# Rows of o of two tiles in one visit across block borders, with finer positions in a planned order

## The chip, the cores and the metric

The kernel runs on one core of a Trainium2 chip. The metric is the device time of one execution in microseconds (us), the median of several runs. A profiled execution has a time of its own; its span, from the first to the last instruction, is a little shorter than that time.

## The reference

Linear attention with a norm by head, and then an MLP with softplus:

```
kv = einsum('bhsd,bhse->bhde', k, v)          # 8 batches, 8 heads, 576 positions, head size 64
o  = einsum('bhsd,bhde->bhse', q, kv)
rms = sqrt(mean(o * o, axis=-1) + 1e-06)
x  = (o / rms * g_norm) -> (4608 tokens, 512)
h  = x @ w_in                                 # 512 -> 2048
out = softplus(h) @ w_out                     # 2048 -> 512
```

q, k, v and g_norm are float32, w_in and w_out float64. The output is float32.

## The kernel before

**Arithmetic.** A float32 matmul is made of fp32r matmuls on three pieces of each operand (a high part, a rest, and a scaled difference). Weights, x and softplus(h) are split into such pieces by ACT and DVE, and TensorE (PE) adds three products in its accumulators.

**Stages.** Tokens come in 36 tiles of 128. A batch has 576 tokens, four and a half tiles, so that some tiles hold rows of two batches.

- `kv_of(b)` loads k and v of one batch and makes kv on PE (L672, five pieces for each batch: four pairs of loads and a tail); ACT copies the result.
- `rows(t)` makes a tile of o. q is turned (by PE at L752 for batches 0 and 1, by DVE at L727 later), PE makes the rows (`out_rows`, L696, 16 matmuls of 64*64 for each tile; the profile counts each twice), ACT squares them (L769), DVE sums (L700), POOL takes the root (L703, L704), DVE multiplies (L708). x is then turned, for the first 12 tiles on PE (`turn_x`, L714) and later on DVE (L795), and stored to DRAM (L779, L799). For the first six tiles, x is also split at once (L616, L619, L622).
- Phase 0 works on 12 blocks of three tiles (384 tokens) and the first chunks of the hidden layer, four chunks of 128 for the first four blocks and six for the others, 64 steps in all. A step has `mm1` (L839, 12 matmuls of 384 columns), softplus (L861), the split into `gv` (L863, L850, L854) and `mm2` (L846, nine matmuls of 512 columns, three for each tile). The partial output goes to DRAM (L891, L906).
- Phases 1 and 2 work on nine blocks of 512 tokens and pairs of chunks, 48 steps in all. They use a form with seven products in place of eight: `units_of` prepares sums of x, `both` prepares sums of weights, `wide_step` has seven products of six matmuls (L1026, 256 columns), the softplus and split (L1053, L1075, L1083, L1086, L1089) and eight `mm2` of three matmuls (L1096). Phase 2 adds the partial outputs of the phases before (L885) and writes the result.
- Weights arrive as float64 and are converted by ACT and six DVE instructions (L414 to L440, with L410 and L427 on ACT), then split (`split_weight`, L477 to L505). Weights that are needed later are spilled to DRAM (L458) and loaded again.

**What sets the order.** The kernel does not issue instructions as the source stands. Each piece of work is a `Task` with an engine, a cost, the tasks it needs, buffers that it takes and gives, and a position. `Plan.order` builds the whole order before anything is issued: on each engine it takes, of the tasks that can start within a small window, the one with the lowest position. So the position is a rank, and the engine's queue is fixed when the program is built. On PE, `rows` and `kv` tasks are of a kind of their own, and the planner keeps tasks of one kind together when several are ready; a small cost is charged for a change of kind. Where PE would stand idle early on, the planner puts in a filler, `warm` (L1177), a matmul on the identity.

A DMA has a `behind`: it is not issued before the mm1 of a given step is. All data DMAs but two are issued from SP.

The lines that the change and the prediction touch:

```
# which tile joins the rows of the tile before it (12 = BY_PE, TB = 3 tiles in a block)
second = t >= BY_PE and t % TB == 1
if second:
    rows_done[t - 1].after.extend(turned + need)
a = o_task = add("PE", 484, out_rows, turned + need, pos - second, [o], [qT], kind="rows", follows=rows_done.get(t - 1))
```

With `second`, the tile before also waits until this tile's q is turned and its kv is there, so that both can be done in one visit. `x_pos(t)` gives a tile's position, `EARLY`, `CONVERT`, `FETCH`, `LATER`, `SPLIT`, `TAKEN` and `MM2` hold the positions and offsets of loads, conversions, splits and matmuls.

Of the kernel before, what the change touches and what calls it, by code (L numbers as in the profile page):

```python
# [18 lines left out]
P = 128  # L19
# [181 lines left out]
def kernel(  # L201
# [44 lines left out]
    STEPS = [(ph, n, p) for ph in (1, 2) for n in range(n_wide) for p in PAIRS[ph - 1][n]]  # L246
    LAST = 2

    P0 = [-48.16, -11.59, -36.23, -9.34, -21.88, -6.03, 0.48, 3.73, -72.34, -30.1, -41.26, -15.18, -39.67, -26.8, -3.81, 5.27, 8.4, -26.81, 14.38, 10.02, 8.24, 12.88, -11.53, 5.44, 1.19, 33.13, -14.12, 6.15, 11.68, 7.45]
    CONVERT, FETCH, EARLY, LATER = P0[:8], P0[8:16], P0[16:27], P0[27:]  # L250
    P1 = [49.25, 55.64, 61.04, 40.09, 109.45, 133.28, 49.73, 28.85, 72.45, 98.22, 131.85, 140.31]
    P2 = [24.13, 36.89, 36.77, 47.57, 55.58, 67.77, 58.81, 116.43, 78.93, 120.62, 44.24, 19.49, 49.95, 77.41, 122.0, 83.32, 80.75, 86.17, 164.23, 141.39, -6.45]
    P3 = [1.62, 1.24, 5.47, 0.83, 2.68, 2.58, 4.22, 2.0, 2.57, 2.99, 3.06, 1.5, 1.16, 0.45, 2.4, -0.72]
# [330 lines left out]
    def load_q(b):  # L584


        q_slots[b], q_loads[b] = slot("qa"), []
        pos = x_pos(first_tile[b] + 1) - EARLY[7]

        def run(a, p):  # L590
            if not (a or p):
                new(q_slots[b], [P, NP * S])
            e, c = divmod(a, 2)
            nc.sync.dma_start(
                out=q_slots[b].tile[BL * a:BL * (a + 1), p * S:(p + 2) * S].rearrange("j (i d) -> j i d", d=BL),
                in_=q[b, e * NP + p:e * NP + p + 2, :, BL * c:BL * (c + 1)].rearrange("p (i j) d -> j (p i) d", j=BL))

        for a in range(4):
            for p in range(0, NP, 2):
                q_loads[b].append(add("SP", 500, lambda a=a, p=p: run(a, p), (), pos + 0.1 * (2 * a + p // 2),  # L600
                                      [q_slots[b]] if not (a or p) else [], [], 1095, behind=int(pos) - 3,
                                      follows=q_loads[b][-1] if a or p else None))

    def split(t, x, ready, pos):
# [33 lines left out]
    def x_pos(t):  # L638

        n = t // TB  # L640
        return t * EARLY[0] + EARLY[1] if n == 0 else first_step["block", n] - (EARLY[2] if n == 1 else EARLY[3]) + t % TB

    def kv_of(b):

        pos = x_pos(first_tile[b]) - (EARLY[4] if b else EARLY[5])
        bank = slot(f"s{b}" if b < 2 else "tp")
        last = first = None
        MAIN = 4 * P  # L650
        for p in range(NP + 1):
# [11 lines left out]
            lds = [add("SP", 500, lambda src=src, s=s, load=load: load(src, s), (), pos - EARLY[6] + 0.5 * p, [s], [],  # L663
                       650 if tail else 850, behind=int(pos - 2) - 3) for src, s in ((k, ks), (v, vs))]

            def run(ks=ks, vs=vs, p=p, tail=tail):
                kv = new(bank, [P, NP, D]) if p == 0 else bank.tile
                for i in range(4):
                    for e in range(2):
                        l, r = (x.tile[:, i + e * NP] if tail else x.tile[:, e, i] for x in (ks, vs))  # L670

                        nc.tensor.matmul(kv[e * D:(e + 1) * D, i if tail else p], lhsT=l, rhs=r,  # L672
                                         start=(p == 0 and i == 0), stop=tail, skip_group_check=True)
            if b >= 2 and (p % 2 or tail):
                first.after.extend(lds)
            last = add("PE", 470, run, lds + ([last] if b < 2 else []), pos + 0.5 * p, [bank] if p == 0 else [], [ks, vs], kind="kv",
                       follows=last if b >= 2 else None)
            if p % 2 == 0 and not tail:
                first = last
        kv_ready[b] = [add("ACT", 400, lambda: nc.scalar.copy(kvs[b % 2], bank.tile), [last] + o_tasks.get(b - 2, []),  # L680
                           pos + 2.5, [], [bank])]

    def rows(t):
# [38 lines left out]
        for b, r0, n, s0 in parts(t):  # L722
            if b >= 2:
                if b not in q_slots:
                    load_q(b)
                turned.append(add(
                    "DVE", 690 if n == P else 420, lambda b=b, r0=r0, n=n, s0=s0: nc.vector.transpose(  # L727
                        out=part_of_qT(n, r0),
                        in_=q_slots[b].tile.rearrange("k (p s) -> k p s", p=NP)[:, :, s0:s0 + n]),
                    q_loads[b], pos - 1, [qT] if not r0 else [], [q_slots[b]], follows=turned[-1] if turned else None))  # L730
                continue

            if 0 not in q_slots:
                q_slots[0] = slot("qa")
            at_qa = n == P and b == 0
            q_s = q_slots[0] if at_qa else slot("n")

            def load(b=b, n=n, s0=s0, q_s=q_s, at_qa=at_qa):
                if q_s.tile is None:
                    new(q_s, [P, NP * S] if at_qa else [P, H, D])  # L740
                for e in range(2):
                    nc.sync.dma_start(out=natural(q_s, at_qa)[:n, e::2], in_=halves(q[b, :, s0:s0 + n], e))  # L742

            def natural(q_s, at_qa):
                if not at_qa:
# [9 lines left out]
            ld = add("SP", 900, load, (), pos - EARLY[7], [q_s] if not at_qa or t == 0 else [], [], 1220 * n // P,  # L755
                     behind=int(pos) - 3, follows=first_load[0] if t and at_qa else None)
            first_load.append(ld)
            a = add("PE", 440, turn_q, [ld], pos - 1, [tp], [q_s])
            turned.append(add("ACT", 590, lambda n=n, r0=r0, tp=tp: nc.scalar.copy(part_of_qT(n, r0), tp.tile[:, :, :n]),
                              [a], pos - 1, [qT] if not r0 else [], [tp], follows=turned[-1] if turned else None))  # L760
        need = [u for pt in parts(t) for u in kv_ready[pt[0]]]
        second = t >= BY_PE and t % TB == 1
        if second:
            rows_done[t - 1].after.extend(turned + need)
        a = o_task = add("PE", 484, out_rows, turned + need, pos - second, [o], [qT], kind="rows", follows=rows_done.get(t - 1))
        rows_done[t] = a
        for pt in parts(t):
            o_tasks.setdefault(pt[0], []).append(a)
# [149 lines left out]

    def units_of(ph, n):

        at = starts[first_of[ph, n]] - LEAD
        held = {}
        for j, us in enumerate(GROUPS):
            pos = at + APART * j - (EARLIER if ph == 1 else 0)
# [79 lines left out]
    def wide_step(k):  # L1004
# [101 lines left out]
        for c in range(2):  # L1106
            for i in range(TW):
                slot_pos = b + PACE + MM2[TW * c + i]
                a2 = add("PE", 700, lambda c=c, i=i: mm2(c, i),
                         [a] + factors_done[1, 2 * p + c] + ([seeds[i]] if i in seeds and not c else []) +  # L1110
                         ([before[i]] if c else []), slot_pos, [mine[i]] if first and not c and ph < LAST else [], [gv] + ([outs[c]] if final else []))
                before[i] = a2
                if last and c:
                    leave(ph, TW * n + i, mine[i], a2, slot_pos)
# [30 lines left out]
    for c in range(KF):  # L1145
        for j in (2 * c, 2 * c + 1):
            if c < OWN:
                pos = CONVERT[j] if c < 4 else LATER[c - 4] + LATER[2] * (j % 2)
                weight(j, pos, FETCH[j] if c < 4 else pos, int(pos) - 3)
# [63 lines left out]
```

## Time and profile before

| | |
|---|---|
| median of 3 runs | 881.16 us (880.52 to 881.33) |
| profiled execution, its own time | 881.73 us |
| its span | 878.6 us |
| granted TensorE clock | 0.998 |
| PE busy | 858.5 us (98%) |
| DVE busy | 704.3 us (80%) |
| ACT busy | 519.5 us (59%) |
| POOL busy | 80.1 us (9%) |
| DMA, mean over the span | 190 GB/s |

An engine's busy time is the union of its instructions; a share is that time over the span. For PE the ends of matmuls are modelled and neighbours overlap, so the times from one start to the next are used where a duration matters. In the timeline, each line has the start, the length, the engine, the source line, what is written and read, and how many equal instructions were merged; the bracket at the end is the idle time before it and what ended it. "Filler" in this document means the matmuls at L1177.

### The profile page before, as it was taken

The numbers are of one execution on the slowest core, as the hardware profiler recorded it, in microseconds if no ns is written. First come the engines' busy times: TensorE is split into PE (matmuls) and PEld (weight loads), VectorE is DVE, ScalarE is ACT, GpSimd is POOL, SyncE is SP. The second block draws the span as 40 slices with busy tenths as digits, with TensorE's granted clock in tenths as the row PEclk, the third lists the DMA queues.
The fourth block names the chain that finished last, engine by engine and source line by source line (L and its number), as shares of the span: only waits on it lengthen the run. The fifth ranks groups of instructions, "written<-read, shape, count | busy, mean of one in ns | idle before, by whom it ended". The sixth has DMA issues, their size and how long they took to land.

```text
span 878.6 us, 16974 instructions
## 1 busy us (share of the span) xinstructions
PE 858.5 (98%) x6463; PEld 757.6 (86%) x6463; DVE 704.3 (80%) x992; ACT 519.5 (59%) x979; POOL 80.1 (9%) x79
## 2 busy tenths in 40 slices
PE   7799999999999999999999999999999999999998
PEld 4578888888898899888988988898888888888996
DVE  6888888887887988898988877789787867787863
ACT  5675555544444467766667645555767654665554
POOL 0442143023113200000000000000000000000000
PEclk9999999999999999999999999999999999999999
DMA  9998999969683774446654645645463743777764
GB/s 252 240 220 207 304 210 254 224 174 226 185 169 125 193 213 137 157 129 205 223 165 140 197 133 175 214 151 174 144 180 120 252 154 125 237 228 222 227 191 129
DMA packets 239633, 167.06 MB, mean 190 GB/s; under 512 B 106304, under 2 KB 198464, under 8 KB 239552
## 3 DMA queue, kind: packets, MB, share of 16 engines
q1 hardware_dynamic: 239392, 165.99, 67.0%
q8 instruction: 50, 0.82, 0.4%
q14 instruction: 31, 0.25, 0.1%
q10 hardware_dynamic: 160, 0.00, 0.0%
HBM read 112.98 MB, written 52.95 MB: 189 GB/s over the span
## 4 chain that ended last, share of the span: by engine, by line
PE 91%; DMA 2%; DVE 2%; ACT 2%; SPq 1%; issue 1%; POOL 0%; DVEq 0%; ACTq 0%
PE banks L1096 30%; PE banks L1026 26%; PE banks L846 15%; PE banks L839 15%; PE banks L696 2%; PE banks L672 2%; DMA raw<-in_moe_w_in_dram 1%; SPq L742 1%; DMA early<-in_q_dram 1%; PE banks L714 1%; DMA loads<-in_v_dram 1%; DVE half L708 0%; ACT w L778 0%; POOL r L704 0%; SPq L661 0%
## 5 line engine op out<-in xcount | busy, mean ns | idle before, releaser
L1096 PE MATMUL banks<-pieces,gv 128*128 128x512 f32 x552 | 173.0, 394 | 0.0
L1026 PEld LDWEIGHTS banks<-units,pieces 128*128 128x128 f32 x1212 | 159.1, 190 | 11.0 <-ACT banks L1071 2.0
L1026 PE MATMUL banks<-units,pieces 128*128 128x256 f32 x1212 | 166.2, 282 | 0.7 <-ACT banks L1067 0.4
L846 PE MATMUL banks<-pieces,gv 128*128 128x512 f32 x576 | 146.4, 397 | 0.0
L839 PE MATMUL banks<-units,pieces 128*128 128x384 f32 x768 | 145.6, 338 | 0.1
L839 PEld LDWEIGHTS banks<-units,pieces 128*128 128x128 f32 x768 | 135.0, 188 | 5.1 <-ACT pieces L505 0.2
L846 PEld LDWEIGHTS banks<-pieces,gv 128*128 128x128 f32 x576 | 105.8, 188 | 20.9
L1096 PE MATMUL banks<-pieces,g_False 128*128 128x512 f32 x276 | 108.3, 392 | 0.4 <-DVE g_False L1089 0.4
L1096 PEld LDWEIGHTS banks<-pieces,gv 128*128 128x128 f32 x552 | 95.1, 189 | 13.4 <-DVE banks L885 0.4
L1086 DVE TENSOR_TENSOR gv<-g_True,gv 128x1024 fp32r<-128x1024 f32 x48 | 58.7, 1223 | 40.9 <-ACT gv L1083 40.7
L861 ACT ACTIVATE half<-banks 128x384 f32<-128x384 f32 x64 | 31.4, 491 | 88.9 <-PE banks L839 86.6
L1096 PE MATMUL banks<-w,gv 128*128 128x512 f32 x216 | 67.7, 394 | 0.0
L1053 ACT ACTIVATE g_True<-banks 128x256 f32<-128x256 f32 x96 | 36.8, 384 | 49.1 <-PE banks L1026 47.9
L704 POOL TENSOR_TENSOR r<-r,half 128x8 f32<-128x8 f32 x36 | 65.1, 1808 | 3.0
L1096 PEld LDWEIGHTS banks<-pieces,g_False 128*128 128x128 f32 x276 | 51.8, 188 | 12.5 <-ACT banks L1071 0.8
L989 DVE TENSOR_TENSOR units<-loads,units 128x1024 fp32r<-128x1024 f32 x42 | 51.2, 1220 | 11.4 <-ACT units L986 11.2
L1089 DVE SCALAR_TENSOR_TENSOR g_False<-gv 128x1024 fp32r<-128x1024 f32 x48 | 58.7, 1224 | 1.4
L1075 DVE TENSOR_TENSOR g_True<-banks,g_True 128x512 f32<-128x512 f32 x48 | 33.1, 690 | 24.8 <-PE banks L1026 18.9
L992 DVE SCALAR_TENSOR_TENSOR units<-units 128x1024 fp32r<-128x1024 f32 x42 | 51.4, 1223 | 1.6
L1083 ACT ACTIVATE gv<-g_True 128x1024 fp32r<-128x1024 f32 x48 | 51.0, 1062 | 1.5
L850 DVE TENSOR_TENSOR gv<-half,gv 128x384 fp32r<-128x384 f32 x64 | 35.1, 549 | 20.3 <-ACT gv L863 19.4
L891 ACT ACTIVATE m<-banks 128x512 f32<-128x512 f32 x72 | 42.2, 596 | 15.4 <-PE banks L1096 9.5
(116 smaller groups left out, 1347.9 us busy)
## 6 DMA issues: line engine op xcount, KB each, us to landing
loads<-x SPq DMA_DIRECT2D x180, 128.0 KB, 2.8
part<-m SPq DMA_DIRECT2D x72, 256.0 KB, 3.0
m<-part SPq DMA_DIRECT2D x72, 256.0 KB, 3.3
loads<-form SPq DMA_DIRECT2D x45, 256.0 KB, 3.0
form<-loads SPq DMA_DIRECT2D x36, 256.0 KB, 2.8
raw<-in_moe_w_in_dram SPq DMA_DIRECT2D x16, 512.0 KB, 5.2
loads<-in_k_dram SPq DMA_DIRECT2D x32, 256.0 KB, 4.9
loads<-in_v_dram SPq DMA_DIRECT2D x32, 256.0 KB, 5.0
```

Of the source, the lines that this page charges most:

```text
L704: nc.gpsimd.tensor_tensor(out=r.tile, in0=r.tile, in1=half, op=ALU.pow)
L839: nc.tensor.matmul(hp, lhsT=w_in.tile[:, i, kd * P:(kd + 1) * P], rhs=xv.tile[:, i, kd], start=(m == 0), stop=(m == 3 * KD - 1))
L846: nc.tensor.matmul(mine[i].tile, lhsT=gv.tile[:, m, i * P:(i + 1) * P], rhs=w_out.tile[:, m], start=(c == cs[0] and m == 0), stop=(c == cs ...
L891: a = add("ACT", 690 if ph == LAST else 600, lambda: nc.scalar.activation(new(ot, [P, d_model]), bank.tile, func=AF.Copy, scale=scale if p ...
L989: nc.vector.tensor_tensor(out=part_of(1, F32R), in0=xl.tile if m > 1 else xl.tile[:, 0], in1=part_of(0), op=ALU.subtract)
L992: nc.vector.scalar_tensor_tensor(out=part_of(2, F32R), in0=part_of(1), scalar=-RADIX, in1=part_of(0), op0=ALU.mult, op1=ALU.add)
L1026: nc.tensor.matmul(place(q), lhsT=w[:, m, at:at + P], rhs=dst.tile[:, m, v, kd] if u < 6 else dst.tile[:, m, kd], start=(u == 0 and not m ...
L1053: nc.scalar.activation(dst, src, func=AF.Softplus, scale=1.0 + E)
L1083: nc.scalar.activation(gvt(0, F32R), gt(), func=AF.Copy, scale=DOWN)
L1086: nc.vector.tensor_tensor(out=gvt(1, F32R), in0=gt(), in1=gvt(0), op=ALU.subtract)
L1089: nc.vector.scalar_tensor_tensor(out=gt(F32R), in0=gvt(1), scalar=-RADIX, in1=gvt(0), op0=ALU.mult, op1=ALU.add)
L1096: nc.tensor.matmul(mine[i].tile, lhsT=(gvt(m, F32R) if m < 2 else gt(F32R))[:, c, i * P:(i + 1) * P], rhs=outs[c].tile[:, m], start=fresh ...
```

## The change

It does three things. First, the rule for which tile joins the one before it: it was the middle tile of each block of three, from tile 12 on; now it is each odd tile from 13 on, so that pairs (12, 13), (14, 15) and so on run across the borders of blocks, and the pair's position is that of its first tile. Second, a tile's position within its block is spread over the block's steps, and lists of offsets are added (`P4` for each tile, `P5` for each batch's kv and q loads, `P6` for each block's units, `P7` for single loads of the first two batches and tiles). All old constants are replaced. Third, three small rules: `behind` of loads is no longer rounded, and in phases 1 and 2 each first `mm2` of a block's step also names the one before it on the same tile of the block as something to wait for.

```diff
+    P4 = [-30.17, -6.08, 16.93, -33.9, ...
+    P5 = [1.24, -5.69, -2.28, 1.58, ...
+    P6 = [-0.39, 4.6, -0.28, -2.24, ...
+    P7 = [-23.78, -17.98, -11.85, ...
-    P1 = [49.25, 55.64, 61.04, 40.09, 109.45, 133.28, 49.73, 28.85, 72.45, 98.22, 131.85, 140.31]
-    P2 = [24.13, 36.89, 36.77, 47.57, 55.58, 67.77, 58.81, 116.43, 78.93, 120.62, 44.24, 19.49, 49.95, 77.41, 122.0, 83.32, 80.75, 86.17, 164.23, 141.39, -6.45]
+    P1 = [48.8, 48.65, 66.31, 74.64, 125.35, 131.27, -11.31, 54.26, 67.75, 469.13, 282.82, 195.86]
+    P2 = [22.14, 35.93, 25.02, 37.31, 52.38, 81.67, 74.61, 116.65, 106.27, 111.35, 100.82, -152.23, 99.52, 221.41, 428.54, -173.95, 119.58, -155.43, 317.87, 212.07, -7.69]
...
-        pos = x_pos(first_tile[b] + 1) - EARLY[7]
+        pos = x_pos(first_tile[b] + 1) - EARLY[7] + P5[B + b]
...
-                                      [q_slots[b]] if not (a or p) else [], [], 1095, behind=int(pos) - 3,
+                                      [q_slots[b]] if not (a or p) else [], [], 1095, behind=pos - 3.5,
...
-        return t * EARLY[0] + EARLY[1] if n == 0 else first_step["block", n] - (EARLY[2] if n == 1 else EARLY[3]) + t % TB
+        return P4[t] + t * EARLY[0] + EARLY[1] if n == 0 else P4[t] + first_step["block", n] - (EARLY[2] if n == 1 else EARLY[3]) + t % TB * (len(CHUNKS[n]) // TB)
...
-        pos = x_pos(first_tile[b]) - (EARLY[4] if b else EARLY[5])
+        pos = x_pos(first_tile[b]) - (EARLY[4] if b else EARLY[5]) + P5[b]
...
-        second = t >= BY_PE and t % TB == 1
+        second = t > BY_PE and t % 2 == 1
         if second:
             rows_done[t - 1].after.extend(turned + need)
-        a = o_task = add("PE", 484, out_rows, turned + need, pos - second, [o], [qT], kind="rows", follows=rows_done.get(t - 1))
+        a = o_task = add("PE", 484, out_rows, turned + need, x_pos(t - second), [o], [qT], kind="rows", follows=rows_done.get(t - 1))
...
-        at = starts[first_of[ph, n]] - LEAD
+        at = starts[first_of[ph, n]] - LEAD + P6[n_wide * (ph - 1) + n]
...
-                         ([before[i]] if c else []), slot_pos, [mine[i]] if first and not c and ph < LAST else [], [gv] + ([outs[c]] if final else []))
+                         ([before[i]] if c or not first else []), slot_pos, [mine[i]] if first and not c and ph < LAST else [], [gv] + ([outs[c]] if final else []))
```

`P0` and `P3`, the remaining lists of positions, get new values in the same way. After the change all source lines below the lists stand four lines lower.

More of the change, by code (lines that the diff above doesn't have):

```diff
@@ L247 @@
     LAST = 2
-    P0 = [-48.16, -11.59, -36.23, -9.34, -21.88, -6.03, 0.48, 3.73, -72.34, -30.1, -41.26, -15.18, -39.67, -26.8, -3.81, 5.27, 8.4, -26.81, 14.38, 10.02, 8.24, 12.88, -11.53, 5.44, 1.19, 33.13, -14.12, 6.15, 11.68, 7.45]
+    P0 = [-45.94, -26.77, -11.8, 0.28, -29.91, -5.64, -2.86, 3.84, -103.4, -98.98, -69.3, -76.66, -68.5, -24.67, -23.22, -34.97, 8.15, -43.02, 7.47, 9.69, 7.18, 18.16, -12.1, 4.75, 1.0, 95.98, -6.45, 6.38, 7.69, 5.17]
+    P4 = [-30.17, -6.08, 16.93, -33.9, -22.35, -28.91, -17.33, -7.12, -9.75, -2.59, 0.87, 2.93, -12.14, -3.26, 0.98, 3.76, 7.8, -3.0, -2.25, 7.68, 20.89, 50.27, -0.5, -0.13, 26.66, 22.67, -11.61, -5.55, 2.74, 0.64, -0.48, 1.34, 0.64, 1.68, -8.4, -1.37]
+    P5 = [1.24, -5.69, -2.28, 1.58, 5.58, 0.43, 5.83, -7.56, 3.01, -2.95, 3.18, 1.42, -14.52, 0.57, -1.29, -1.34]
+    P6 = [-0.39, 4.6, -0.28, -2.24, -0.01, 1.05, 1.77, -3.9, -2.15, 0.85, 1.85, -1.74, 6.34, -2.44, -0.13, 3.82, 7.89, 0.51]
+    P7 = [-23.78, -17.98, -11.85, -14.93, 0.41, 1.61, 7.35, 2.7, -25.02, -6.6, -15.2, -4.48, -2.14, 0.64, 2.93, 0.97, 4.67, 5.36, 3.33, 6.57, -10.37, 2.36, -14.11, -9.89, -7.11, 12.91, -2.89, 14.55, 12.59, 9.35]
     CONVERT, FETCH, EARLY, LATER = P0[:8], P0[8:16], P0[16:27], P0[27:]
-    P1 = [49.25, 55.64, 61.04, 40.09, 109.45, 133.28, 49.73, 28.85, 72.45, 98.22, 131.85, 140.31]
-    P2 = [24.13, 36.89, 36.77, 47.57, 55.58, 67.77, 58.81, 116.43, 78.93, 120.62, 44.24, 19.49, 49.95, 77.41, 122.0, 83.32, 80.75, 86.17, 164.23, 141.39, -6.45]
-    P3 = [1.62, 1.24, 5.47, 0.83, 2.68, 2.58, 4.22, 2.0, 2.57, 2.99, 3.06, 1.5, 1.16, 0.45, 2.4, -0.72]
+    P1 = [48.8, 48.65, 66.31, 74.64, 125.35, 131.27, -11.31, 54.26, 67.75, 469.13, 282.82, 195.86]
+    P2 = [22.14, 35.93, 25.02, 37.31, 52.38, 81.67, 74.61, 116.65, 106.27, 111.35, 100.82, -152.23, 99.52, 221.41, 428.54, -173.95, 119.58, -155.43, 317.87, 212.07, -7.69]
+    P3 = [3.0, 2.86, 5.84, -16.31, 1.53, 3.03, 3.55, -20.64, 3.15, 2.55, 1.38, 1.52, 1.27, 0.75, 2.42, -1.39]
     SPLIT = {p: (P1[i], P1[6 + i]) for i, p in enumerate((2, 3, 4, 5, 6, 7))}
@@ L661, in load @@
                 nc.sync.dma_start(out=new(s, [P, 2, 4, D]), in_=src[b, p::NP, :MAIN].rearrange("h (s i) d -> s h i d", i=4))
-            lds = [add("SP", 500, lambda src=src, s=s, load=load: load(src, s), (), pos - EARLY[6] + 0.5 * p, [s], [],
-                       650 if tail else 850, behind=int(pos - 2) - 3) for src, s in ((k, ks), (v, vs))]
+            lds = [add("SP", 500, lambda src=src, s=s, load=load: load(src, s), (), pos - EARLY[6] + 0.5 * p + (P7[2 * (5 * b + p) + of_v] if b < 2 else 0), [s], [],
+                       650 if tail else 850, behind=pos - 5.5) for of_v, (src, s) in enumerate(((k, ks), (v, vs)))]
             def run(ks=ks, vs=vs, p=p, tail=tail):
@@ L754, in rows @@
             tp = turn_q.__defaults__[-1]
-            ld = add("SP", 900, load, (), pos - EARLY[7], [q_s] if not at_qa or t == 0 else [], [], 1220 * n // P,
-                     behind=int(pos) - 3, follows=first_load[0] if t and at_qa else None)
+            ld = add("SP", 900, load, (), pos - EARLY[7] + P7[20 + t], [q_s] if not at_qa or t == 0 else [], [], 1220 * n // P,
+                     behind=pos - 3.5, follows=first_load[0] if t and at_qa else None)
             first_load.append(ld)
@@ L1148 @@
                 pos = CONVERT[j] if c < 4 else LATER[c - 4] + LATER[2] * (j % 2)
-                weight(j, pos, FETCH[j] if c < 4 else pos, int(pos) - 3)
+                weight(j, pos, FETCH[j] if c < 4 else pos, pos - 3.5)
             else:
```

## The prediction

> **What bounds the kernel now.** I read the page's busy times first, then busy time by stage, then PE's timeline and its waits.
>
> ```profile
> PE 858.5 (98%) x6463; PEld 757.6 (86%) x6463; DVE 704.3 (80%) x992; ACT 519.5 (59%) x979; POOL 80.1 (9%) x79
> ```
>
> ```profile
> 0.00:48.00 48.00, 34.61 (x429) 24.74 (x430) 35.89 (x64) 29.54 (x58) 10.16 (x15) 0.96 0.96 244
> 48.00:78.00 30.00, 28.69 (x330) 23.92 (x329) 26.17 (x45) 19.52 (x40) 11.22 (x10) 1.00 0.88 228
> 78.00:364.00 286.00, 285.50 (x2536) 253.21 (x2536) 238.15 (x409) 155.19 (x304) 58.67 (x54) 1.00 0.79 195
> 364.00:875.00 511.00, 509.68 (x3171) 455.73 (x3169) 404.07 (x477) 314.81 (x581) 0.00 (x0) 1.00 0.58 180
> ```
>
> The columns are stage, length, busy time of PE, PEld, DVE, ACT, POOL, then clock, DMA share, GB/s. From 78 us to the last matmul PE idles 0.50 + 1.32 = 1.8 us of 797. There the end is the sum of what PE is given, and another engine counts only if it makes PE wait. Before 48 us the DMA share is 0.96 and PE is idle for 13.4 us; also, part of its "busy" time is filler (L1177, 18.2 us in all, a matmul on the identity that the planner puts into gaps).
>
> What PE's small jobs cost shows in start-to-start times (start, length, operation):
>
> ```profile
> 176.62 2.26 PE L846 MATMUL banks<-pieces,gv 128*128 128x512 f32 x9
> 178.82 1.16 PE L696 MATMUL banks<-early,w 64*64 64x64 f32 x64
> 179.91 2.37 PE L839 MATMUL banks<-units,pieces 128*128 128x384 f32 x12
> 182.12 2.24 PE L846 MATMUL banks<-pieces,gv 128*128 128x512 f32 x9
> 184.20 2.27 PE L839 MATMUL banks<-units,pieces 128*128 128x384 f32 x12
> ...
> 271.61 4.35 PE L839 MATMUL banks<-units,pieces 128*128 128x384 f32 x24
> 275.89 0.69 PE L696 MATMUL banks<-early,w 64*64 64x64 f32 x32
> 276.52 2.36 PE L839 MATMUL banks<-units,pieces 128*128 128x384 f32 x12
> 278.72 4.33 PE L846 MATMUL banks<-pieces,gv 128*128 128x512 f32 x18
> ```
>
> L846 x9 lasts 2.08 us when L839 follows (182.12 to 184.20), but 2.20 when rows of o (L696) follow; L839 x12 lasts 2.21 after a visit, 2.10 elsewhere. Two tiles in one visit (x64) take 1.09, one tile (x32) 0.63. So a visit costs 0.10 on entry and 0.11 on exit: one tile 0.84 us, two tiles 1.30, and **two singles made one save 2 x 0.84 - 1.30 = 0.38 us**; with 0.62 for a single, the commoner value, 0.35. I take 0.35.
>
> The waits on PE after 78 us are four short ones:
>
> ```profile
> PE banks L696 <- ACT half L769: 0.4, 1, 0.4
> PE banks L1026 <- ACT banks L1067: 0.4, 1, 0.4
> PE banks L1096 <- DVE g_False L1089: 0.4, 1, 0.4
> PE banks L1026 <- ACT g_True L1050: 0.3, 1, 0.3
> ```
>
> The start-up, PE's timeline:
>
> ```profile
> 44.70 0.69 PE L672 MATMUL banks<-loads 128*64 128x64 f32 x16 [1.17 <-DMA loads<-in_v_dram]
> ...
> 47.12 0.69 PE L696 MATMUL banks<-early,w 64*64 64x64 f32 x32
> 47.74 2.36 PE L839 MATMUL banks<-units,pieces 128*128 128x384 f32 x12
> ...
> 60.88 0.73 PE L1177 MATMUL banks<-ident_r 128*128 128x512 f32 x2
> 62.49 0.66 PE L714 MATMUL banks<-ident_r,half 128*128 128x128 f32 x4 [0.88 <-ACT half L769]
> ```
>
> The first mm1 (L839) stands at 47.74, behind the last kv of batch 1, which waited for DMA until 44.70. After it fillers and waits still take 1.61 us (60.88 to 62.49), 0.92 and 0.33 us (until 77.53) and 0.16: 3.0 in all.
>
> **What the Trainium skill says.** "TensorEngine Tiling (Array Packing)", Key Properties: changing the tiling mode drains TensorE. The trace agrees: rows run as 64*64 between 128*128 work, and the two changes cost the 0.10 and 0.11 us above. "TensorE: Matmul & The Clock Gate", section "Wait — 56ns, not 53.3ns?", gives 215.7 ns between 512-column matmuls; here 2.10 / 9 = 233 ns, and I use that. "DMA: Bandwidth & Descriptors", "Why small descriptors are slow", names a fixed cost per packet. The trace agrees; two short stretches of DMA, q-heavy (12.1 to 14.0 us) and nearly without q (14.8 to 19.0):
>
> ```profile
> DMA packets 1005, 0.40 MB, mean 209 GB/s; under 512 B 811, under 2 KB 1005, under 8 KB 1005
> ...
> DMA packets 1189, 1.48 MB, mean 352 GB/s; under 512 B 121, under 2 KB 1068, under 8 KB 1189
> ```
>
> **The change part by part.**
>
> *Rows of o.* In the built instruction order of both kernels I count runs of L696 on PE. All 36 tiles take 28 visits before, 23 after. The last 27 tiles (from tile 9 on), which lie in the part where PE never idles, take 20 visits before and 16 after: 4 x 0.35 = **-1.4 us**. Tiles 2 and 3 are merged too, but ahead of the first mm1, where PE idles: 0. Tile 5's visit moves ahead of the first mm1; that takes 0.83 from the work after it and adds it to the start-up. What is late next is ACT's Square of both tiles, two of 0.60 us back to back; two o slots hold both.
>
> *Other PE work.* mm1, mm2, products, kv visits (20) and x transposes (12 visits) are equal in number. Runs of product and wide mm2 number 171 and 168 before, 170 and 169 after. I priced all runs from the first mm1 on by the durations above: 821.5 us before, 819.1 after, difference 2.4: 1.4 + 0.83 and 0.2 of small moves. (The measured stretch, 47.74 to 874.74, is 827.0 = 821.5 + 3.0 + 1.8 + 0.7 unassigned.)
>
> *Start-up loads (SP's queue, DMAs included).* Both kernels move the same 10.24 MB up to the last k and v of batch 1. But before, two q tiles (7 and 8, 2 x 256 KB) stand ahead of them, and after, w_in of chunk 3 (512 KB) stands there. At 209 and 352 GB/s: 2.5 against 1.5 us. So that kv is ready near 43.7 instead of 44.7. Behind it after: kv 1.1, q transpose 0.4, rows 0.7, x transpose 0.45, rows 0.65, six fillers of 0.33: first mm1 at about 49.1, **+1.35 us** against 47.74. From there on two fillers (0.66) remain, and I expect about 1.0 of waiting for tile 4's x (6.7 us from its rows to its transpose in the trace of before, 47.12 to 53.78): 1.7 instead of 3.0, **-1.3 us**. The kinds of both terms are sure, their sizes to 1 us each.
>
> *DVE.* The first g-split ends (L854) as the 85th DVE instruction, not the 74th: 11 more, about 7.1 us at 0.45 to 0.73 each. DVE before has done that much at about 62 us. PE after reaches the mm2 that needs it at about 63.5 us. So it is hidden, with 1.5 us to spare; beyond that it costs one for one.
>
> *Loads' gates, weight conversions, units, the added order among mm2 runs in phase 2.* All are positions in queues. The added dependency holds PE against PE, which is in order anyway: 0. Nothing is added to or taken from DVE (992 both) or ACT. The longest DVE work between two g-splits falls from 9.8 to 7.8 us in the 384-token part and from 15.9 to 11.3 in the 512-token part (counts by row durations), which speaks for no new wait. The 1.8 us of waits after 78 us may vanish or double: +-1.8; I take 0.
>
> Sum: -2.4 + 1.35 - 1.3 = **-2.35 us**. The profiled execution took 881.73 us (878.6 of span, 3.1 around it), so 879.4 for it; the median of the runs is 0.57 lower, 881.16, so **878.8**. The tail (last matmul 874.74, ACT 0.69, store, end 878.6) doesn't change.
>
> **The rivals.** (1) *As above*, 877.8 to 879.9, chance 0.46: within it the start-up terms move by 1 us. (2) *The waits after 78 us go too*: -2.35 - 1.8 = 877.0. For it: the one of 0.43 at 188 us lies between single visits, of which there are fewer. Against: three are in the 512-token part or near the end, which is hardly reordered. Chance 0.20. (3) *The start-up gives it back*: the DMA advance isn't there (+1.0) or DVE's 11 instructions come out late (1 us); only the visits are left or less: 880 to 881, no measurable change. For it: DVE is 75% busy before 48 us, 87% until 78. Chance 0.27. (4) *Slower*: the conversions of weight chunks 7, 11 and 13 get positions far below zero, so that each weight's six DVE instructions (0.43 + 3 x 0.69 + 0.43 + 0.69 = 3.6 us) run as soon as it lands, ahead of a waiting g-split. PE's cover is one mm1 and one mm2, 4.2 us, less ACT's and DVE's 2.1 us for the split itself: 2.1 us. Above that PE waits; six such weights at 1.5 us, half of them hit: +4.5 - 2.35, so 883.3. Against it: the shorter stretches above. Chance 0.07. That the change doesn't do what it says is excluded by the count 28 to 23.
>
> **How the numbers follow.** A measurement of this kernel can tell about 0.2% (1.76 us) from no change, so faster means under 879.4. Case 2 is faster whole, of case 1 nearly all (0.43), case 3 is the same with a little of case 1, case 4 slower. Faster 0.64, same 0.29, slower 0.07. The range takes in cases 1 to 3: 876.8 to 881.1.
>
> **What would show it.** Right: L696 in 16 visits from tile 9 on, each double 1.09; first mm1 near 49; last filler before 79 us; PE idle after that under 2 us. Wrong: waits of PE on DVE at L846 (case 3 if at 60 to 65 us, case 4 if between 80 and 360), or a last kv of batch 1 still at 44.7.

## The result and the profile after

The changed kernel takes **874.38 us** (median of four runs, 873.61 to 875.38); the kernel before took 880.84 us on the same chip (four runs, 880.11 to 881.33). The ratio is 0.9928, 95% interval 0.9911 to 0.9945: faster by 6.5 us. I had forecast 878.8 us with a range of 876.8 to 881.1. The sign was right; the size was not, and the range missed.

The profiled execution took 873.68 us, with a span of 871.7 us and a granted clock of 0.994. The time around the span was 2.0 us, and it was 3.1 us in the profiled execution before; therefore I compare spans and positions inside them, not the two profiled times.

The busy times of the page after:

```profile
PE 858.2 (98%) x6464; PEld 761.2 (87%) x6464; DVE 703.9 (81%) x992; ACT 521.4 (60%) x979; POOL 78.3 (9%) x79
```

PE's busy time is that of before to 0.3 us, although the span is 6.9 us shorter. As a total it says nothing about the change: fillers are in it, and the modelled ends of matmuls cover short stalls. The stages say more (stage, length, busy time of PE, PEld, DVE, ACT and POOL, then clock, DMA share, GB/s):

```profile
0.00:48.00 48.00, 39.95 (x471) 29.91 (x472) 38.33 (x69) 31.68 (x61) 11.62 (x18) 0.89 1.04 264
48.00:78.00 30.00, 28.54 (x358) 23.74 (x357) 25.80 (x45) 20.46 (x41) 10.95 (x12) 1.00 0.95 238
78.00:364.00 286.00, 286.00 (x2494) 254.94 (x2493) 243.19 (x417) 156.72 (x309) 55.73 (x51) 1.00 0.81 197
364.00:868.00 504.00, 503.75 (x3147) 452.62 (x3145) 396.55 (x464) 311.91 (x570) 0.00 (x0) 1.00 0.57 179
```

From 78 us on PE idles 0.25 us, where it idled 1.8. The list of waits, which had four entries for PE in that stretch, has none. Before 48 us DVE does 38.33 us of work, 2.4 more than before, and DMA moves 264 GB/s, not 244.

Visits of rows of o are as counted: 16 from tile 9 on. A double one in PE's timeline (start, length):

```profile
72.80 1.16 PE L700 MATMUL banks<-early,w 64*64 64x64 f32 x64
73.89 2.35 PE L843 MATMUL banks<-units,pieces 128*128 128x384 f32 x12
```

From start to start that is 1.09 us, as in the kernel before. The start-up in the same timeline:

```profile
40.85 0.69 PE L676 MATMUL banks<-loads 128*64 128x64 f32 x16
...
45.35 1.66 PE L1181 MATMUL banks<-ident_r 128*128 128x512 f32 x6
46.85 2.27 PE L843 MATMUL banks<-units,pieces 128*128 128x384 f32 x12
```

The last kv pair of batch 1 (L676) no longer waits for a DMA and stands at 40.85, where I expected 43.7. The six fillers are there as predicted, and the first mm1 (L843) stands at 46.85, not at 49.1 as predicted, nor at 47.74 as before.

**Where the time came from.** I take PE's timeline from start to start and price each run of equal matmuls by the durations in the prediction. What is left over in a stretch is waits and fillers. This account of one profiled execution is called its ledger below.

| | before | after | difference | predicted |
|---|---|---|---|---|
| first mm1 starts at | 47.74 | 46.85 | -0.89 | +1.35 |
| PE work from there on, priced | 821.53 | 819.08 | -2.45 | -2.4 |
| fillers and waits until 78 us | 3.34 | 3.02 | -0.32 | -1.3 |
| left over, 78 to 364 us | 0.46 | -0.22 | -0.68 | 0 |
| left over, from 364 us | 1.67 | -0.84 | -2.51 | 0 |
| last matmul ends at | 874.74 | 867.88 | -6.86 | -2.35 |

The negative values are the error of the prices, about 1 us in 790. With prices taken anew, as medians over several of the traces, the two left-over terms come out as -0.3 and -2.8: their sum, 3.1 to 3.2 us, is firm, and how it divides between the two stretches is known to about 0.4. The work term is the count of the built order at the same prices as in the prediction, so its agreement shows no more than that the order was counted rightly; the price of a visit is tested in e12 below. The term that I had set to zero holds 3.2 us, and the start-up 1.2 us (first mm1 and fillers together) where I had a sum of zero.

The 2.5 us from 364 us on lie in the runs of product and of wide mm2 (L1030, L1100). By the ledger five stalls of the kernel before, at 84, 187, 368, 675 and 684 us, hold 2.6 of the 3.2 us; the changed kernel has none over 0.2 us there. Two of the five, each in its run (in the bracket the idle time and its releaser):

```profile
373.79 0.98 PE L1026 MATMUL banks<-units,pieces 128*128 128x256 f32 x6 [0.41 <-ACT banks L1067]
...
676.29 2.41 PE L1026 MATMUL banks<-units,pieces 128*128 128x256 f32 x18 [0.26 <-ACT g_True L1050]
```

Around the first, 60 matmuls of product took 7.82 us from start to start, 0.67 more than their price; the bracket shows 0.41. The second names 0.26, and its run of 72 lost 0.56. After the change, products stand back to back from the first one on:

```profile
362.49 3.02 PE L1030 MATMUL banks<-units,pieces 128*128 128x256 f32 x24
365.35 1.58 PE L1030 MATMUL banks<-early,w 128*128 128x256 f32 x12
```

### The profile page after: what moved, and what is told of

The parts are those of the page before. It is cut to its first block, busy times and chain, and to the rows that moved or that the text cites. A ratio compares the mean times of both kernels' runs of the same rounds, so it can differ in the third digit from the quotient of the medians.

```text
span 871.7 us, 17016 instructions
## 1 busy us (share of the span) xinstructions
PE 858.2 (98%) x6464; PEld 761.2 (87%) x6464; DVE 703.9 (81%) x992; ACT 521.4 (60%) x979; POOL 78.3 (9%) x79
## 4 chain that ended last, share of the span: by engine, by line
PE 94%; DMA 2%; DVE 2%; ACT 1%; POOL 1%; issue 0%; SPq 0%; POOLq 0%; DVEq 0%; ACTq 0%
PE banks L1100 30%; PE banks L1030 28%; PE banks L850 16%; PE banks L843 15%; PE banks L700 2%; PE banks L676 2%; DMA loads<-in_k_dram 1%; DMA loads<-in_v_dram 1%; PE banks L1181 1%; PE banks L718 0%; POOL r L708 0%; DVE half L712 0%; PE banks L756 0%; SPq L403 0%; DVE units L623 0%
## 5 line engine op out<-in xcount | busy, mean ns | idle before, releaser
L1100 PE MATMUL banks<-pieces,gv 128*128 128x512 f32 x696 | 217.9, 394 | 0.0
L843 PE MATMUL banks<-units,pieces 128*128 128x384 f32 x768 | 145.8, 338 | 0.0
L850 PE MATMUL banks<-pieces,gv 128*128 128x512 f32 x576 | 145.5, 396 | 0.0
L843 PEld LDWEIGHTS banks<-units,pieces 128*128 128x128 f32 x768 | 135.1, 188 | 5.1
L1100 PEld LDWEIGHTS banks<-pieces,gv 128*128 128x128 f32 x696 | 121.2, 189 | 18.1
L1100 PE MATMUL banks<-pieces,g_False 128*128 128x512 f32 x348 | 136.4, 392 | 0.1
L1030 PEld LDWEIGHTS banks<-units,pieces 128*128 128x128 f32 x948 | 126.9, 190 | 8.3 <-ACT banks L1075 1.3
L1030 PE MATMUL banks<-units,pieces 128*128 128x256 f32 x948 | 132.5, 282 | 0.0
L850 PEld LDWEIGHTS banks<-pieces,gv 128*128 128x128 f32 x576 | 106.3, 187 | 21.0
L1100 PEld LDWEIGHTS banks<-pieces,g_False 128*128 128x128 f32 x348 | 65.4, 188 | 15.3 <-DVE g_False L1093 0.6
L1030 PEld LDWEIGHTS banks<-units,w 128*128 128x128 f32 x396 | 52.5, 189 | 2.8
L1030 PE MATMUL banks<-units,w 128*128 128x256 f32 x396 | 54.8, 281 | 0.0
L990 ACT ACTIVATE units<-loads 128x1024 fp32r<-128x1024 f32 x42 | 44.4, 1058 | 17.0 <-PE banks L1030 11.0
```

The source lines that it names most:

```text
L843: nc.tensor.matmul(hp, lhsT=w_in.tile[:, i, kd * P:(kd + 1) * P], rhs=xv.tile[:, i, kd], start=(m == 0), stop=(m == 3 * KD - 1))
L850: nc.tensor.matmul(mine[i].tile, lhsT=gv.tile[:, m, i * P:(i + 1) * P], rhs=w_out.tile[:, m], start=(c == cs[0] and m == 0), stop=(c == cs ...
L990: nc.scalar.activation(part_of(0, F32R), xl.tile if m > 1 else xl.tile[:, 0], func=AF.Copy, scale=DOWN)
L1030: nc.tensor.matmul(place(q), lhsT=w[:, m, at:at + P], rhs=dst.tile[:, m, v, kd] if u < 6 else dst.tile[:, m, kd], start=(u == 0 and not m ...
L1100: nc.tensor.matmul(mine[i].tile, lhsT=(gvt(m, F32R) if m < 2 else gt(F32R))[:, c, i * P:(i + 1) * P], rhs=outs[c].tile[:, m], start=fresh ...
```

## The experiments

All were timed in five rounds beside the kernel before. Two kinds were made. In the first the planned order is kept and single tasks are moved in it. In the second one part of the positions is set back, or put alone into the kernel before, and the whole is planned again. Below, "start-up" is the start of the first mm1 plus fillers and waits until 78 us: 51.08 before, 49.87 after. Ledgers are of the profiled executions. In the cuts of code, "..." marks what is left out, and the comments are added.

### What a visit costs

**e12_visits_split.** The changed kernel in its own order; wherever a main PE task follows a double visit from tile 12 on, the second tile's rows go behind that task.

```diff
-    for t in plan.order():
+    planned = plan.order()
+    tasks = list(planned)
...
+    for one, two, then in zip(on_pe, on_pe[1:], on_pe[2:]):
+        if one.kind == two.kind == "rows" and then.kind == "all" and then.pos is not None and rows_at[id(two)] >= 12:
+            trial = [t for t in tasks if t is not two]
+            trial.insert(trial.index(then) + 1, two)
...
+    for t in tasks:
```

> The order of the changed kernel is kept, except that the second tile of each double visit from tile 12 on is moved behind the next main PE task: visits of rows from tile 9 on 16 -> 24, nothing else changes place. Theory V (a visit costs 0.35 us and nothing hides it): 8 x 0.35 = +2.8 us on the 874.4 of the changed kernel, 877.2, with PE's waits after 78 us still near none. Rival W (what matters is what else the joint positions do, a visit is free because PE's queue absorbs it): 874.4 to 875.0. Rival X (moving the second tile later makes x late or its buffer late): above 878.5, with PE waits on ACT or DVE in 78 to 364 us.

877.78 us (876.44 to 878.81), ratio to before 0.9956 (0.9944 to 0.9969), against 0.9928 for the changed kernel: 2.5 us of the gain are gone. The eight places can be timed directly. One of them in the changed kernel, and the same work in e12:

```profile
104.08 1.16 PE L700 MATMUL banks<-early,w 64*64 64x64 f32 x64
...
106.67 2.24 PE L843 MATMUL banks<-units,pieces 128*128 128x384 f32 x12
```

```profile
104.24 0.69 PE L701 MATMUL banks<-early,w 64*64 64x64 f32 x32
...
105.76 0.69 PE L701 MATMUL banks<-early,w 64*64 64x64 f32 x32
...
107.19 2.27 PE L845 MATMUL banks<-units,pieces 128*128 128x384 f32 x12
```

From the first rows to the mm1 it is 2.59 us with one visit and 2.95 with two. Over the eight places, the same work takes 0.34 to 0.38 us longer at each, 2.90 in all; the prices give 2.84 (821.92 from 819.08). Besides, 1.1 us more is left over between 78 and 364 us, by the ledger. **Theory V holds**: a visit has its price, and nothing hides it.

**e13_visits_merged.** The kernel before in its own order; in two places the main tasks between two single visits are moved behind the second.

> The order of the kernel before is kept on every engine, except that in two places PE's main tasks between two single visits are moved behind the second, so that two pairs of singles become two doubles: visits from tile 9 on 20 -> 18. Theory V: -2 x 0.35 = -0.7 us on the 880.9 of the kernel before, 880.2, ratio 0.9992. Rival W (a visit is free): no change. Rival X (the mm1 and mm2 moved behind let their consumers wait): slower, with a new PE wait after 78 us.

883.67 us, ratio 1.0022 (1.0009 to 1.0034): slower. The priced work falls by 0.71 us, which is the count of visits, but 4.6 us of waits came between 78 and 364 us. PE's timeline at one of the two places, and its waits after 78 us (total, times, longest):

```profile
284.67 0.69 PE L697 MATMUL banks<-early,w 64*64 64x64 f32 x32
286.88 0.69 PE L697 MATMUL banks<-early,w 64*64 64x64 f32 x32 [1.51 <-ACT half L771]
```

```profile
PE banks L697 <- ACT half L771: 1.9, 2, 1.5
PE banks L697 <- DVE half L709: 1.5, 1, 1.5
```

The second tile's rows now stand directly behind the first's, and wait 1.5 us for ACT or DVE on an earlier tile, whose Square (L771) and multiplication (L709) read o. The mm2 that had covered this wait (at the other place an mm1) stands behind it. X holds: far more is lost than the visits are worth where nothing else was moved. At these two places a double visit would pay only if the tiles before it were finished with. In the changed kernel no double visit after 78 us shows a wait.

### What bounds the start-up

**e9_six_fillers_out** leaves the six fillers ahead of the first mm1 out, **e10_no_fillers** all 52 of them. Both keep the changed kernel's order.

```diff
+    while on_pe[at - 1].pos is None:      # a filler, directly ahead of the first mm1
+        at -= 1
+        left_out.add(id(on_pe[at]))
```

```diff
-        t.run()
+        if t.pos is not None:
+            t.run()
```

> The order of the changed kernel is kept, but the six filler matmuls just ahead of its first mm1 (45.35 to 46.85 us) are left out. The data of that mm1 are there at 43.64 us. Theory F (fillers that stand in a ready queue delay the main work): the first mm1 starts at 45.3 to 45.5, and of the 1.5 us up to 1.0 comes out at the end, because the next task that waits for DVE or ACT (the turn of x at 48.6 us) takes back some: 873.2 to 874.0. Rival G (the start-up is bound by DVE's and ACT's chain up to 78 us, so PE waits later by what it gained): 874.4, with the same sum lost up to 78 us.

> The order of the changed kernel is kept, but no filler matmul is issued at all. Theory F: PE's main tasks start when their data are there, as in the run with six left out, and the fillers after it (2 single ones, 1.0 us) turn into waits: 873 to 874.4. Rival H (fillers keep the clock of TensorE up): the granted clock before or after 48 us falls and the time rises by 1 us or more, above 875.5.

873.80 us (873.31 to 874.30) and 875.13 us (873.92 to 875.50); neither can be told from 874.38. In e9 the first mm1 starts at 46.22, 0.63 earlier, and then stops within itself:

```profile
46.22 1.68 PE L843 MATMUL banks<-units,pieces 128*128 128x384 f32 x8
48.33 0.97 PE L843 MATMUL banks<-units,pieces 128*128 128x384 f32 x4 [0.43 <-DVE units L626]
```

Its last four matmuls wait for DVE's last x-split. Fillers and waits until 78 us grow from 3.02 to 4.35. **Rival G holds**, F falls: the fillers stood in a wait that was there anyway. Of rival H, half came: without fillers the granted clock is lower in each of the five executions (0.989 to 0.992, against 0.994 to 0.997 in the four of e9 and the four of the changed kernel). In the profiled one it is 0.67 and 0.74 from 20 to 40 us, and 1.00 from 40 us on. The time above 875.5 us did not come; e10's median is 1.3 us above e9's on the same chip, but their executions overlap.

**e14_q_behind** and **e15_q_ahead** move loads alone. e14 is the kernel before with q of tiles 7 and 8 behind the last three loads of batch 1's k and v; e15 is the changed kernel with q of tile 7 ahead of the last four.

```diff
+    on_sp = [t for t in planned if t.engine == "SP"]
+    group, goal = on_sp[32:34], on_sp[36]      # e14, put behind the goal
+    group, goal = on_sp[36:37], on_sp[32]      # e15, put ahead of the goal
```

> The kernel before, its order kept, but on SP the loads of q of tiles 7 and 8 (four DMAs that took 5.30 us to issue from 32.79 us) are moved behind the last three loads of k and v of batch 1. The same bytes are moved. Theory Q (the DMAs of 256-byte pieces hold up what is queued behind them by more than the 2.5 us that I priced): the last kv of batch 1 starts at 41.5 to 42.5 instead of 44.70, the first mm1 at 45 to 46.5 instead of 47.74, and 0.5 to 1.5 us come out at the end: 879.4 to 880.4. Rival G (up to 78 us a later chain through ACT and DVE decides, not the first mm1): first mm1 earlier, the time the same, 881. Rival P (my price of 1 us was right): first mm1 at 46.5 or later.

> The changed kernel, its order kept, but on SP the load of q of tile 7 (two DMAs, 2.13 us to issue) is moved ahead of the last four loads of k and v of batch 1. Theory Q: the last kv of batch 1 starts at 42.5 to 43.5 instead of 41.37, the first mm1 at 48 to 49 instead of 46.85, and 0.5 to 1.5 us more at the end: 875.0 to 876.0. Rival G: first mm1 later, the time the same, 874.4.

e14: 881.60 us, ratio 1.0 (0.999 to 1.0011). e15: 874.02 us (873.61 to 875.85), ratio 0.9921 (0.9905 to 0.9937). Neither changes the time. e14's timeline:

```profile
36.68 1.13 PE L696 MATMUL banks<-early,w 64*64 64x64 f32 x32
...
43.64 0.69 PE L672 MATMUL banks<-loads 128*64 128x64 f32 x16
...
46.22 0.66 PE L714 MATMUL banks<-ident_r,half 128*128 128x128 f32 x4 [0.56 <-ACT w L778]
...
47.67 2.38 PE L839 MATMUL banks<-units,pieces 128*128 128x384 f32 x12
```

The last kv pair of batch 1 starts 1.06 us earlier than the 44.70 of before, and waits for no DMA. The first mm1 starts where it did, 47.67 against 47.74: the gain is lost to waits on ACT and DVE, of which 0.56 us at the turn of x (L714) on ACT's L778. In e15 that kv starts at 41.54, 0.7 later (the expectation's 41.37 is its tail), and nothing comes of it. So **G holds again**. Theory Q falls. The last load of v ahead of this kv was issued 2.7 us earlier in e14 (37.20, from 39.91), near the 2.5 us that I had priced for the two tiles of q; the kv gained only 1.06 of it, because other work on PE, with a wait of 0.34 us for DVE in it, then stood ahead of it, and the first mm1 nothing.

The next views are DVE's waits before 48 us, first of the kernel before, then of the changed one:

```profile
DVE m L414 <- DMA raw<-in_moe_w_in_dram: 4.9, 3, 2.6
```

```profile
DVE m L418 <- DMA raw<-in_moe_w_in_dram: 2.0, 2, 1.7
```

DVE converts weights that arrive from DRAM, and it waits 2.9 us less for them in the changed kernel. It has done 2.1 us more by 78 us (64.13 from 62.06, from the sums of its busy time). This fits a start-up bound by DVE and ACT, but that the weights' earlier arrival is what brought the start-up's gain was not isolated: in e14 DVE waited 1.6 us less for weights too (3.3), and the time stayed. The size of the gain is not certain either. The start-up order of the changed kernel also ran in five more kernels (e12, e5, e17 and e18, and e15 with one load moved), and with the changed kernel's own 49.87 the start-ups are 49.87 to 50.95, mean 50.3. With the old order (the kernel before, e13, e6, e14 with its loads moved) they are 50.26 to 51.20, mean 50.9. By the means the gain is 0.6 us. Among these runs, those with every start-up load in its place (the changed kernel, e12, e5, e17, e18, against the kernel before, e13 and e6) show once more that the first mm1 does not hang on the kv: by the means the last kv of batch 1 starts 2.9 us earlier (41.6 from 44.5), and the first mm1 0.2 us (47.3 from 47.5).

### Parts of the change by themselves

**The pairing rule: e1_pair_undone and e2_pair_alone.** e1 is the changed kernel with the old rule, e2 the kernel before with the new one (the reverse edit).

```diff
-        second = t > BY_PE and t % 2 == 1
+        second = t >= BY_PE and t % TB == 1
...
-        a = o_task = add("PE", 484, out_rows, turned + need, x_pos(t - second), ...
+        a = o_task = add("PE", 484, out_rows, turned + need, pos - second, ...
```

> The changed kernel with the old pairing rule (middle tile of each block), all new positions kept. From tile 9 on rows of o take 18 visits on TensorE, against 16 with the new rule and 20 before the change. Theory A (the gain is a sum of parts, and a visit is worth its 0.35 us): 2 x 0.35 = 0.7 us slower than the changed kernel, 875.1 us. Theory B (the pairing is what makes the gain, since it also takes pressure from the two o slots and so removes the waits after 78 us): at least 2.5 us slower, 877 us, and waits of TensorE on ACT or DVE after 78 us come back in the trace.

> The kernel before with the new pairing rule alone. From tile 9 on 18 visits instead of 20. Theory A: -0.7 us, 880.1 us, with the waits after 78 us still near 1.8 us. Theory B: -2.5 us or more, 878.3 us, with those waits gone.

e1: 885.46 us, ratio 1.0049 (1.0034 to 1.0063). e2: 890.22 us, ratio 1.0098 (1.008 to 1.0116). Both have 18 visits from tile 9 on, and both are slower than the kernel before. With only two visits between them and either kernel, the price of a visit can't explain 9 to 11 us. In e1, 10.8 us are left over between 78 and 364 us; the largest single wait is at rows:

```profile
237.30 1.13 PE L709 MATMUL banks<-early,w 64*64 64x64 f32 x32 [4.32 <-DVE half L721]
```

In e2 most of the loss lies elsewhere: 8.8 us more than before are left over from 364 us on, the longest waits being of products for ACT, and the start-up took 2.5 us more in its profiled execution, the slowest of its six. The expectations missed, since they took the rest of the order to stay as it is. It doesn't: in the programs as built, e1's order differs from the changed kernel's on every engine.

**The start-up's positions: e3_start_undone and e4_start_alone.** The positions of the first six tiles, two batches and four weight chunks are old in e3 (the rest as changed) and new in e4 (the rest as before).

```diff
+        new_, early = (S_NEW, EARLY_S) if t < 6 else (M_NEW, EARLY_M)
+        own = P4[t] if new_ else 0
```

> The changed kernel with the start-up's positions (tiles 0 to 5, k and v of batches 0 and 1, weights of chunks 0 to 3) as before the change. 18 visits from tile 9 on; 12 fillers stand behind the first mm1, against 2. Theory A: the start-up's share is the earlier first mm1 (0.9 us), tile 5's visit ahead of it (0.8) and 0.3 of waits, with 0.7 for two visits: 2.7 us slower than the changed kernel, 877.1 us. Theory C (the start-up carries most of it, since TensorE is full afterwards and each us of the start reaches the end): 5 us slower, 879.4 us.

> The kernel before with the start-up's new positions alone (old pairing). 19 visits from tile 9 on instead of 20. Theory A: -2.0 for the start and -0.35 for a visit: 878.5 us, first mm1 near 47. Theory C: -5 us, 875.8 us.

e3: 904.73 us, ratio 1.026 (1.0241 to 1.0279), with 22.0 us left over between 78 and 364 us, where nothing was edited. e4: 880.68 us, ratio 0.9995 (0.9986 to 1.0005): the new start-up positions alone give the kernel before nothing (its start-up is 51.24).

**The 512-token part: e5_wide_undone and e6_wide_alone.** Here the order of the 384-token part is kept. e5 is the changed kernel with old `P3`, no `P6` and the old rule for the first mm2 of a step; e6 is the kernel before with the new ones.

> The changed kernel with the old positions of the 512-token part alone (old P3, no P6, the old rule for the first mm2 of a step); its order up to the end of the 384-token part is that of the changed kernel. Theory S (of the 3.2 us of PE waits that went after 78 us, the ones at 368, 675 and 684 us in the trace of before belong to these positions): those three come back, +1.9 to +2.5 us: 876.3 to 876.9, and nothing is lost before 364 us. Rival R (positions that were chosen together can't be mixed): several waits of 2 us or more after 364 us, above 879. Rival N (the waits follow from what the 384-token part leaves behind): no change, 874.4.

> The kernel before with the new positions of the 512-token part alone; its order up to there is that of the kernel before. Theory S: the waits at 368, 675 and 684 us go, -1.9 to -2.5 us: 878.5 to 879.2. Rival R: new waits after 364 us, above 883. Rival N: no change, 880.9 to 881.4.

e5: 878.99 us (876.77 to 881.77), ratio 0.9976 (0.9964 to 0.9988): 4.2 us of the gain are gone by the ratios. 1.8 us are left over in the first run of products (it starts at 363.24) and 3.5 more than in the changed kernel after 364 us, some 2 us of it in runs at 414 to 417, 485 and near 680 us. e6: 893.48 us, ratio 1.0143 (1.0122 to 1.0163). 12.0 us more than before are left over after 364 us, 8.6 of them in one run of products, which waits in several places, longest here:

```profile
412.66 0.50 PE L1039 MATMUL banks<-turned,half 128*128 128x256 f32 x2 [3.83 <-ACT turned L999]
```

Theory S had the kind right in e5 and half the size: stalls come back in the first run of products and near 680 us, close to places that it named, but also at 417 and 485 us, which it did not. It fell in e6 (rival R). The stalls of the kernel before do not belong to the positions of that part by themselves: the new ones take them away behind the new 384-token part, and make far worse ones behind the old.

**e17_units_undone and e18_p3_undone** ask which of the two lists it is. e17 takes `P6` as zero, e18 has the old `P3`; the rest is the changed kernel. The third edit, the added order among mm2 runs, needed no run: with and without it the built program is the same, instruction by instruction.

```diff
-        at = starts[first_of[ph, n]] - LEAD + P6[n_wide * (ph - 1) + n]
+        at = starts[first_of[ph, n]] - LEAD
```

```diff
-    P3 = [3.0, 2.86, 5.84, -16.31, 1.53, 3.03, 3.55, -20.64, ...
+    P3 = [1.62, 1.24, 5.47, 0.83, 2.68, 2.58, 4.22, 2.0, ...
```

> The changed kernel with P6 (the offsets of single units of each block of 512 tokens) taken as zero, P3 new; the 384-token part is the same. With all positions of the 512-token part old, 4.6 us came back. Theory J (the units are what was late for the products that waited, at 363, 417 and 485 us): at least 2.5 us of PE waits come back behind the units or turns of x, 877 to 879. Rival K (P3, the places of the mm2 runs, decides): under 1 us, 874.4 to 875.4. Rival R (mixed positions lose more than all old ones): above 879, with one wait over 3 us at the first blocks.

> The changed kernel with the old P3 (the places of the mm2 runs and of the split of g in the 512-token part) and the new P6. Theory J (the units decide): under 1 us, 874.4 to 875.4. Rival K (P3 decides): 2.5 us or more, 877 to 879, waits behind ACT's softplus or DVE's split of g. Rival R: above 879, because P6 was chosen with the new P3.

e17: 879.92 us, ratio 0.9977 (0.9965 to 0.9988). e18: 879.38 us, ratio 0.9965 (0.9951 to 0.9978). 5.1 and 4.5 us more are left over after 364 us than in the changed kernel. e17 at its first products:

```profile
369.59 0.50 PE L1030 MATMUL banks<-units,pieces 128*128 128x256 f32 x2 [0.75 <-DVE units L993]
370.92 1.22 PE L1030 MATMUL banks<-units,pieces 128*128 128x256 f32 x8 [0.83 <-DVE units L996]
```

The products of the first block are there before DVE has made the sums of x that they read. So neither J nor K holds: one list alone undone loses about as much as both (4.3 and 3.3 us by the ratios, against 4.2), and the lists work only together. R holds in kind, not in its size: set against the kernel before on the same chip both lie under 879, and no wait reaches 3 us. This also means that these losses are of mixed positions; how much of the 2.5 us of gain after 364 us each list brings can't be read from them. No experiment gave a version that can be told from the changed kernel on the fast side.

## Why the prediction was right or wrong, point by point

- **Rows of o: right.** 16 visits from tile 9 on and 1.09 us for a double; e12 shows eight visits at 0.34 to 0.38 us each, where I had 0.35. The sum of PE work, -2.4, came out as -2.45, by the same prices.
- **First mm1, +1.35 us: wrong in sign, -0.89 in the profiled execution, -0.2 by the means.** The step that failed is the chain "kv of batch 1, then 1.1 + 0.4 + 0.7 + 0.45 + 0.65 and six fillers". It had two errors in what it rests on, and a third in its size. The kv stood at 40.85, not 43.7: I had compared only the loads that stand ahead in one place and what they move, while the whole queue had advanced (the first kv at 8.51 us instead of 10.56, DMA 264 against 244 GB/s before 48 us). And the kv is not what the first mm1 hangs on: e14 moved it by 1.06 us and the mm1 by 0.07; e9 took the fillers out, and the mm1 then waited for DVE's split. And the time from that kv to the mm1 was 6.00 us (40.85 to 46.85), where the chain had 5.4 (43.7 to 49.1), since two waits on DVE and ACT, of 0.23 and 0.62 us, stand in it.
- **Fillers and waits until 78 us, -1.3 us: mis-sized, -0.32.** This and the last term are one quantity, since what is gained ahead of the first mm1 is waited for behind it. Together I had zero; measured is -1.2, of which by the means over several kernels 0.6 can be counted on.
- **DVE's 11 more instructions: right.** The first mm2 did not wait for its g-split; there is no PE wait on DVE at L850 at 60 to 65 us.
- **The added order among mm2 runs, 0: right.** It changes nothing in the built program.
- **Waits after 78 us, 0: wrong, -3.2 us. This is the main error.** I had read 1.8 us of idle PE and taken them as likely to stay, "may vanish or double". They vanished, and they were larger than they looked: a stall shorter than the modelled overlap of two matmuls is counted as busy, so that 0.41 us of bracket stood for 0.67 us of loss. My case 2 had the mechanism, at 0.20 and with 1.8 us. The argument against it, that the 512-token part is hardly reordered, was false: that part has its own new lists, and undoing one or both of them costs 3.3 to 4.3 us by the ratios, though partly in new waits of its own.
- **Range.** Its low end was case 2 beside a start-up that gains nothing. Measured by the ledger, case 2's 3.2 and the start-up's 1.2 came together, 4.4 us, and the cases had never been added up. The range left the joint one out.
- **Slower, by conversions with very low positions: did not come.** No PE wait stands between 80 and 360 us.

What stays open: which single moves made the start-up shorter, and which removed the 0.3 to 0.7 us between 78 and 364 us, though part of it is the wait of 0.4 us for ACT at 188 us, which is gone. Whether the old positions of the 512-token part alone made its stalls stays open too, since undoing them brought other ones. Positions set back in parts made new waits of 4 to 22 us in seven of eight runs (e4 is the exception), which hide effects of this size.

## What to carry to other kernels

In a kernel with a planned order, add up PE's work from one start to the next by runs of equal instructions; from 78 us on such prices met the measured stretch of the changed kernel to about 1 us in 790, and what is left over is the whole of the waits, more than the idle columns show. A change that sets all positions anew can take all of it at once, as here, so the range has to reach there. And a part of jointly chosen positions is not tested by setting it back: keep the built order and move the few tasks in question.

## What the runs showed of the hardware that was not expected

The granted clock of TensorE can fall for a while in the start-up, and not in each execution: from 30 to 40 us it was 1.00 in the kernel before and 0.66 in e14, which has the same PE order. There a tile of rows took 1.13 us in place of 0.69 (36.68 in e14's timeline). Nothing of it is seen at the end: the first mm1 starts at 47.67 in e14 and at 47.74 in the kernel before, and from 78 us on the clock was 1.00 in both. Without fillers, as e10 shows, the mean clock was lower in each execution, by 0.002 to 0.008 of full speed against any of e9's, and again no longer time is shown.
